# A long-convolution and linear-memory attention kernel on one core: another stored order of the same operations, with other PSUM banks and eviction engines

## The chip, the core and the metric

The kernel runs on one core of a Trainium2 chip. The core has a matrix engine (PE, which loads weights on a path of its own, PEld), a vector engine (DVE), a scalar engine (ACT), GpSimd (POOL), and a sync engine (SP) that here only issues transfers. PE writes its results to PSUM, eight banks of 512 fp32 columns on 128 partitions; DVE or ACT must evict them to the on-chip memory before a bank is used again. Each engine takes its instructions strictly in the order in which the program lists them, and waits where an operand isn't ready. The metric is the device time of one execution in microseconds (us), less is better.

## What is computed

Two layers that share nothing but the launch; their results are joined along the last axis (2048 x 1280).

```python
# A: a four-tap filter on k, times v, then a causal convolution over 2048 steps (by FFT), times q
k_shift = sum of k_pad[:, t:t + S] * shift_k[:, ks - 1 - t]
kv = k_shift * v
y  = irfft(rfft(kv, 4096) * rfft(ssm_k, 4096))[:S] + kv * ssm_D
a  = q * y
# B: 32 heads of 20, four segments of 512 steps, causal softmax inside a segment and a linear memory across
q, k, v = x @ wq, x @ wk, x @ wv
for s in range(4):
    a_dot = softmax(qs @ ks.T * scale + mask) @ vs
    a_mem = (phi(qs) @ M) / (phi(qs) @ z + 1e-6)
    o = g * a_mem + (1 - g) * a_dot
    M, z = M + phi(ks).T @ vs, z + sum(phi(ks))
b = o @ wo
```

## The kernel before

Layer A is cut into five blocks of 128 channels (`conv(dp)`). For each block the filter `ssm_k` and the product `kv` are brought into layout, taken through a discrete Fourier transform by matmuls with the table `Wf` (`spectrum`: eight PSUM groups "FK" for the filter and eight "FX" for kv), combined and multiplied on DVE (`product`, tiles F, Kh, Xh, pq, Y), and taken back by matmuls with `Wi` (`inverse`). The four taps are matmuls too, with diagonal weight tiles `skd`, 20 small products that ACT makes once from the `taps`. Layer B runs in eight units u: a segment s = u // 2 and a half of the heads. `project(u)` makes keys and queries (KQ, groups "P") and values (Va, groups "V") with the weights `wqkv`, transposes them by DMA into KQT, and bounds the scores (kam, A, qabs, and four "rows" transfers). `attend(u)` makes score tiles in PSUM ("S": A, D and J for the parts of the causal triangle, D the diagonal one), evicts them with an Exp on ACT into one of seven tiles ET, multiplies them by the values ("O") and normalises on DVE (rr, o2, o_s). `project_out(s)` multiplies by `wo` and stores. x's first segment is loaded in four quarters (Y_97 in the program's names) that PE transposes ("xt") into xT; the later segments are transposed by DMA. Ten warm-up matmuls on zeros stand first on PE.

None of this runs in the order of the code. A recorder (`Recorder`) takes each call as an operation with its predecessors: 1505 operations, 471 PSUM groups. `issue` then sends them out in the order of a stored table `ORDER`; `BASE` gives each group its first bank, and `EVICT`, a string of 227 digits, says for each plain eviction whether DVE ("1") or ACT ("0") does it (`evict`). So three tables decide what stands on each engine's list, and which bank a matmul waits for; nothing is scheduled at build time. All instructions are sent out from one line, L261, so the profile tells them apart by their tiles.

SP issues 201 transfers, GpSimd four (the constants `pack`, `shift_k`, `beta` and `ssm_D`).

Of the kernel before, what the change touches and what calls it, by code (L numbers as in the profile page):

```python
# [21 lines left out]
S = 2048; D = 640  # L22
H = 32; DH = 20; NS = 4; L = 512
# [246 lines left out]
class Layer:  # L270
# [134 lines left out]
    def evict(self, out, in_, grp):  # L405
        e = self.evicts
        self.evicts += 1
        if EVICT[e] == "1":
            self.nc.vector.tensor_copy(out=out, in_=in_, grp=grp)
# [506 lines left out]
    def project_out(self, s):  # L916
# [41 lines left out]
        for t in range(4):  # L958
# [31 lines left out]
SKA = (0, 1, 2, 3, 4)  # L990
KQV, QN = 0, 4
TAP2 = (3, 4)
EVICT = ("10100001110000001000000010000000000000000000000000000000000000100000000000001000010001001010100110100000000000000000110000000000000010000000"
         "000000000101000100100100000000000000010000001100001000000000000000000000010110010000100")
KQW, FW, WW = 1, 1, 1
ORDER = r"""
c-jrtgMttW5Czb=Gk0=rwrjI(+um&3wry{=YqM?Jwr#$5zT#w+Y?57aNKVNmxh0R}l_(NXTtrGs6^SI}q@v`L>Jn9=NgOF7p(MXlmGV+nk_aWQR+7{bAQdE|RFeV{Sqe%KEhI&?uv8XEKCPs6rKXsuRMxIiTWU#W
Ni5MNro@oa8cWJ(eyt%v(p?H@LP;gXw2qY3G*Vw`YC~x*^`x9;k=D{uifcCs(gxB<+DZ!vEw!|<l$177TboKh=^^bTtyIx;Qc-(J9c?9bwU0EBdfH6VOM5A$9i^(ql_FAH3Tl6;p*^Lr_LjcVLCWhO=_CWBn8cG|
l3cpT2<a@brG(Vi1d>RGNJA|u4K%C_mN7C=hRY~PDPd%s43)7mTB>OyEupJ*yo{6yQb>b!gErRcx<}S%d?~3-wTaHry|PjlX$tA4$t076lL|UfR%vscB$H)|?2`~(tW#yPY?AI;N@mDL-7l?lnrzbPazK`751p$s
rL`{AHabt6X<PlJEwsHJm6qB;=W9EiC0pg7bkd&MOBZNIJtlp1wj7qux=jwrHr=jAq__6bwc16y>Kxgj+hv^|my6O*Pe`!r)M2_=FUeI|p$m1m_SY>sK(EPMiDM&lr^K~gx>YaBX_+VEb-rAYcy>mX%Pxs(6Lp|2  # L1000
kli{#<J%57FN1WCuGif%Mx$A38>fq8uP&6NwnZ+;GTo<R^{gzG!MaSA>p3~5`!%Jdv7tIdPs&n>k5rb-qT6vjpp$f(PS;a1QV(i)nXEDFzKqsUn%Ex7bD5$`WQNYv>oQeu$qKn4H|4e**2j{>?#L{CDR<?NX0{`m
!B)#reIT<n0UpU~c_nM)jjWVJc2QqQR768Uq_DTLN)jQXWwQ11L@wz&$zoUZvOblha!sE}R@)$JB{9-lcDt&lb)CGIVV1)_N-`uzY&)w@bhw?-50V5S@>DlUPCKE`^ppl7DRS8-IjK`@gq_o=Hqr)KbX?FBh#<H1
yymvg5(9ZHrp2<<_#$bM#|GIqiHSS<Q19wjNrUV9NMqr#-q4$x4!884=CeMCjkkJVze|35pg&~1^|v^9r|<QZCbzU!!0yQ}iHiZ26|XhWe##roh<JFeza^bzLT3Dx43f>p+8>!<FSMY&)C86dAM}g<laKmU$5=uO
g-@CVpS7fY(}_0DfYO#8-!(J@KeUu(fFV03SxV$U8B2wqTGkZPtgscbB38+!8&S?8ps4jjWgBJ1tcp1zA}2;$aVuf7E!YNIE_A{Wt7>5|%Vt;}6h}3yZecOgCR+*Au-qt$APa|@79Qm-5{hAt<;7g9VEIrUg;5rz
QPE0bp1ri%))xVoZ-G+BDxe(dS`jR?0jOuStPB=eJ1d3yRuBQ~U_&iG8rV8pZ0)VJ^+!WnZ(t!Tu`rCxwicUhOxeOJVyO*8SjJ%#4na$+gk`qeMxd2d!3vAYMm7kQF%-iv5-V+i4Mt;YYE8`eTZf}6R#`QWG1=V4
U>us+Sj6H6tAUL+9^n`n9j%jvXJ-qs1YB)vY^`;%C@@RNuJ%{E8LczA+g9sg|Fox7M=$Gb+pLd?ZMXRB&P42Mn=A<va|$+FKXZ#j*cR)CP!@xCFqFG3G?TI)doTinFpSB$$EKn`yJG_O+78=i1+d?0;(-0piHOKR
*2Y1L#va&ZJFN@i@{mPmEhOU^i^qHDz&^Z-!`2gZ(3L58&d%B;>&trR#*`d|RJ>xBZ5q<B7mnHt)W<P9V#n=-rDjLY#7V1*(Ku!2tv9Bl0WMlZYY68gq-AKkV4>I*H!K~S;-=lQ!3?nG7{c2Y+3uKHW8AgLxM%Hn
)goDYUbFjXg!IhJ>z0uN*pv5dEHiOAnxGj@+hWYZ1AAnT?THQIQ=5%B2xFr-kip2pUR;9VoQs9%#0;E=wFqmYxdJ1&2wC~edb2Yh+Ip<R7`8)pF2xf(w`^R7hse!w+<<3zfc6;Ayd24ie2Ud*fjnG^HCTm7e2yG!
gPhF8`MANB$j1c;L4HnV7q-F_w#6k}Mr%x^djW>>f}GAG6feZ0gim8(7Go6Kh#7og#aW4=eI{REGfJ>BH=zpuvLv^lBevotI-mx__&5Gz5P$GHtFk74avQ4gJxg-}w__H|uq?~*Bdhb3T|q6DVtIbx96rJhd}19|
U@))ZG3K&1>vA?Dcmp<MBhF(*?!+}T<~O`S6E<aie!(vMVLgVk>-dhhXvRg{jfNi4!`oMUwi{^97Hr8@T+Hykg!8!vk-Rl;;<bITM*h*%7jgk3`&Yh#`7N~JC+x#gwq<*#f3nwjhbSK8x3Qe-xEB#@89R7XU(cGp  # L1010
9~&6L6?~7+*vMn}fK{yJoA?o{xsnI4mSH`bH}i0Q5NmiGwLQAOvwdvt@9hWnv%VkTQT)Ua1b7VJ%q`r?ZQRZV9@7uwAY=I<9O7ZN^&Q;FuNK=|czoZ@Jv@QE{DseK=dN-5H;(Wx{@@D(^dwsPQ6A$dgwns3*#F_p
{}GDkyLcM^40?)@HHp8qq#oDLK((uzez4O#i{tF#)Dt|zvka>z+0D-}wAS-5dY(NziiX#4n!qD!R6U2D9zoCJ7ZZ6Tji$-`0u%ZV>*W{O*?%*-CikBf=$CkzSD3<6`EN_<S9y(ptc~aQ>x`+ry^mi+L2v3Yw6Ul5
0^ZNRSsG90!t|cOGkR=|rD^@UHSs*2*ZX=t&*c5Rm1p(=UdV5<h+n`XX7y~I-Q#Kw&*FtWr^nG>*4m5uV?N+*=JMiR!i)Js-r^v?!%{xPOM4kF>*YM2j`Nb9+XwmtkFR%G-k-375BBl?ibMS#6KW;D&(}<#!@aUs
@$O#HhxrJv>Q7n66KN8y<|BQSKjUamtj}53$9Q$`=t;GcPxRC})?aXnPxVRulGA*;FZap*hRJk>ukac^(--<m-|ve(xz6@rpW}1=Ef4q-Po=Ybk*CzXo>7;28lC6!eV?!O6q-|)`38T-OuF7fe4{V$O&+MZbd_)R
b-u+9`XNuN>2$T{(af4&*Z5Z7=2>;S@9=E8(|7r9&!C5Wk00@io<(!(ZNKD4J-Z(B9D2s@_+7u}_x-G&^YebeFZ&h0>eu|b-|(A$%a8jBKk29ZwEqW|<?eI
"""
BASE = r"""
c-mc30kQ=l2qH7P|Bb%^HT(YTw3QJeIRFd<sz+jRy?dN_c64=g_q;oTp3i@FZ1$>p9(|HVZ-8vexIrYy61*|F0uj5v$#^nzP{qkt%qZ3%W{_Dok{Dq(H71#r0akn%z}00Jclvx$gQ@^)TGSeh?zfxH6-23;AWyw`
GIDlB{xWvhS!ov&h=r?#|M|G__KO;hF6kM(S=4$QIhkND<bo948P26xGGo5nVNc4hxwzjS4d5wUc|FGXSBGkq=gZwN=<DsC!5i{ii1N6e#&bEJpTGK5VbBdR*N<D$R8}UvVRi9&tDtL19a6U4NyYE>db(@z-nc&e
zj<yB_0_Fy+ZU-_pF7vVd_53;{d!F5fS_B_eBS8~RvQK@  # L1020
"""


# [69 lines left out]
```

## Time and profile before

| | us |
|---|---|
| runs before, median of 3 | 269.18 (268.61 to 269.23) |
| profiled execution, its span (the only time of it that the page has) | 266.3 |
| mean granted TensorE clock, share of full | 1.000 |
| moved by DMA | 41.84 MB, 157 GB/s on average |

A page of the profile shows one execution. Its parts used below are the busy time of each engine, the chain of work that ended last (followed back from the last instruction to what released it), groups of instructions by tile, and the list of instructions in order of time, merged where equal ones follow each other: start, length, engine, operation, output and input with their shapes, and in brackets the idle time before and what ended it. In the chain's list, each row is a start, a length, an engine and the tile written. An instruction's own length is longer than the distance to the next start on the same engine where they overlap.

### The profile page before, as it was taken

Reading aid. Unit: us, or ns where it says so; the run is one execution under the profiler, and the core shown is the slowest. Engines: PE = TensorE matmul, PEld = TensorE weight load, DVE = VectorE, ACT = ScalarE, POOL = GpSimd, SP = SyncE. Lnnn points to the kernel's source line nnn. Section 1 sums busy time; section 2 is a strip of 40 time slices with the busy share of each in tenths; the row PEclk is TensorE's granted clock in tenths of the full one; section 3 lists DMA queues with packets and bytes.
Section 4 is the critical chain, followed back from the end, with each engine's and each line's share of the span. In section 5 each row is a group of like instructions: output and inputs, shape, how many; then the busy total and the mean of one; then the engine's idle time right before and its main releaser. Section 6 shows DMA issues by size and latency. Waiting matters only on the chain.

```text
span 266.3 us, 10034 instructions
## 1 busy us (share of the span) xinstructions
PE 257.8 (97%) x4323; PEld 193.0 (72%) x4323; DVE 247.1 (93%) x387; ACT 248.8 (93%) x392; POOL 7.6 (3%) x20
## 2 busy tenths in 40 slices
PE   7999999999999999999999999999999999988994
PEld 3788678778777778877767777778776876665871
DVE  0599999999999999999999999999999999999971
ACT  2878999999999999999999999999999999999953
POOL 8300000000000000000000000000000000000000
PEclk9999999999999999999999999999999999999999
DMA  7999898999989797996999699958990099345034
GB/s 217 292 214 218 197 180 187 126 233 205 172 200 175 142 180 162 173 154 126 154 173 201 164 185 182 211 107 113 181 186 3 29 158 149 87 108 128 28 66 116
DMA packets 126604, 41.84 MB, mean 157 GB/s; under 512 B 114107, under 2 KB 125376, under 8 KB 126432
## 3 DMA queue, kind: packets, MB, share of 16 engines
q1 hardware_dynamic: 126416, 41.07, 80.1%
q8 instruction: 34, 0.56, 0.9%
q0 software_dynamic: 144, 0.13, 0.1%
q14 instruction: 10, 0.08, 0.1%
HBM read 11.96 MB, written 5.24 MB: 65 GB/s over the span
## 4 chain that ended last, share of the span: by engine, by line
PE 62%; ACT 28%; DVE 5%; issue 2%; DMA 1%; POOL 0%; DVEq 0%; ACTq 0%; POOLq 0%
PE ps L261 62%; ACT ET L261 19%; ACT F L261 3%; ACT KQ L261 1%; ACT PP L261 1%; DMA qabs<-in_A_shift_k_dram 1%; ACT Va L261 1%; DVE vt L261 1%; ACT outb L261 1%; DVE Y L261 1%; DVE Kh L261 1%; ACT qabs L261 1%; DVE pq L261 0%; ACT xT L261 0%; DVE o L261 0%
## 5 line engine op out<-in xcount | busy, mean ns | idle before, releaser
L261 ACT ACTIVATE ET<-ps 128x1024 bf16<-128x1024 f32 x160 | 162.6, 1122 | 0.4 <-PE ps L261 0.2
L261 PEld LDWEIGHTS <-xT 128*128 128x128 bf16 x640 | 57.3, 98 | 27.8 <-issue 6.8
L261 PE MATMUL ps<-wqkv,xT 128*128 128x320 bf16 x480 | 77.0, 299 | 0.4
L261 ACT CAST F<-ps 128x512 bf16<-128x512 f32 x72 | 43.3, 686 | 0.9 <-DVE F L261 0.8
L261 PE MATMUL ps<-Va,ET 128*128 128x21 bf16 x1280 | 41.8, 173 | 0.0
L261 PEld LDWEIGHTS <-ET 128*128 128x128 bf16 x1280 | 39.1, 96 | 2.1 <-issue 1.0
L261 PE MATMUL ps<-KQT 32*128 32x128 bf16 (+3 forms) x896 | 35.7, 239 | 0.3
L261 PEld LDWEIGHTS <-Wf 128*128 128x128 bf16 x320 | 29.8, 98 | 6.1 <-issue 1.3
L261 ACT CAST KQ<-ps 128x320 bf16<-128x320 f32 x54 | 25.5, 513 | 2.4 <-PE ps L261 2.3
L261 PE MATMUL ps<-wo,xT 128*128 128x320 bf16 (+2 forms) x160 | 25.5, 299 | 1.3 <-ACT ET L261 1.3
L261 PEld LDWEIGHTS <-KQT 32*128 32x128 bf16 (+1 forms) x896 | 16.1, 92 | 9.9 <-issue 8.2
L261 PE MATMUL ps<-kT,Wf 128*128 128x256 bf16 x160 | 21.8, 273 | 0.1
L261 PE MATMUL ps<-vt,Wf 128*128 128x256 bf16 x160 | 21.2, 273 | 0.0
L261 PE MATMUL ps<-Y,Wi 128*128 128x256 bf16 x160 | 20.8, 273 | 0.0
L261 DVE TENSOR_TENSOR o<-ps,rr 128x640 bf16<-128x640 f32 x24 | 19.7, 819 | 0.4
L261 DVE TENSOR_TENSOR Y<-Y,pq 128x2048 bf16<-128x2048 bf16 (+1 forms) x20 | 18.6, 937 | 0.0
L261 PE MATMUL ps<-Mbd,PqT 128*128 128x84 bf16 x96 | 18.3, 203 | 0.1
L261 DVE TENSOR_TENSOR pq<-Xh,Kh 128x2048 bf16<-128x2048 bf16 x15 | 18.2, 1215 | 0.0
L261 PE MATMUL ps<-skd,kr 128*128 128x128 bf16 (+4 forms) x124 | 17.9, 270 | 0.0
L261 PEld LDWEIGHTS <-kr 128*128 128x128 bf16 x124 | 15.6, 147 | 2.5 <-issue 0.8
L261 PEld LDWEIGHTS <-Wi 128*128 128x128 bf16 x160 | 14.8, 98 | 2.5 <-issue 0.6
L261 ACT ACTIVATE PP<-KQ 128x1280 bf16<-128x1280 bf16 x12 | 15.9, 1361 | 0.0
(87 smaller groups left out, 355.6 us busy)
## 6 DMA issues: line engine op xcount, KB each, us to landing
vt<-in_A_v_dram SPq DMA_DIRECT2D x10, 256.0 KB
pq<-in_A_q_dram SPq DMA_DIRECT2D x10, 256.0 KB
kT<-kT SPq DMA_DIRECT2D x32, 64.0 KB
out_dram<-pq SPq DMA_DIRECT2D x8, 256.0 KB
out_dram<-outb SPq DMA_DIRECT2D x12, 160.0 KB
Wf<-c_wf SPq DMA_DIRECT2D x4, 256.0 KB
Wi<-c_wi SPq DMA_DIRECT2D x1, 1024.0 KB
kb<-kr SPq DMA_DIRECT2D x4, 256.0 KB
```

What stands on the lines that cost most here:

```text
L261: f(*[fix(a) for a in args], **{k: fix(v) for k, v in kw.items()})
```

## The change

The tables `ORDER` and `BASE` are replaced and 52 of the digits in `EVICT` flip. No operation, shape or transfer is added or removed.

```diff
-EVICT = ("10100001110000001000000010000000000000000000000000000000000000100000000000001000010001001010100110100000000000000000110000000000000010000000"
-         "000000000101000100100100000000000000010000001100001000000000000000000000010110010000100")
+EVICT = ("01111110100100010010010000000000000000000000000000000000000000000000000000000000001010010100100000110000000000000000010000000000000000100000"
+         "000000000010100110100100001000010010000000000000111000000000001000100100000100000001010")
```

Of the flipped evictions 28 go from ACT to DVE: of 512 columns 7 of F, 2 of kT and 2 of the last output rows (PP); of 320 columns 5 of KQ, 4 of Va and 5 of outb; and 3 of x's quarters (640). 24 go from DVE to ACT: of 512 columns 8 of F and one each of kT, PP, qabs and xT; of 320 columns 6 of KQ and 5 of outb; and the taps (40). 390 of the 471 groups get another first bank. On every engine most operations stand elsewhere. On SP the head of the list was the first weights (wk, first half), the identity and x's quarters 0, 3, 1, 2; it now is the identity, x's quarters 3, 1, 2, 0, and then the first weights; the filter of block 0 follows in both, and the pieces of Wf and the other weights change places behind it. GpSimd's four transfers keep their sequence at the front (pack, shift_k, beta, ssm_D); its fills around them change places.

Where the prediction speaks of the start, ACT's list is this. Before (ps is PSUM; skd the diagonal tiles; A and rr the two Exps of beta; kT the filter of block 0):

```order
L261 ACT_TABLE_LOAD
L261 ACTIVATE skd_75<-ident,taps 128x128
L261 CAST xT_95<-ps 128x5x128
L261 ACTIVATE skd_77<-pack,taps 128x64
L261 CAST xT_95<-ps 128x5x128
L261 ACTIVATE A_93<-ps 128x32
L261 ACTIVATE rr_94<-ps 128x32
L261 CAST xT_95<-ps 128x5x128
L261 CAST KQ<-ps 128x16x20
L261 CAST kT_99<-ps 128x2x2x128
```

ACT's list at the same place now, from the table load on:

```order
L261 ACT_TABLE_LOAD
L261 COPY taps<-ps 128x40
L261 ACTIVATE skd_77<-pack,taps 128x64
L261 ACTIVATE skd_78<-pack,taps 128x64
L261 ACTIVATE skd_76<-ident,taps 128x128
L261 ACTIVATE rr_94<-ps 128x32
L261 ACTIVATE skd_76<-ident,taps 128x128
L261 ACTIVATE A_93<-ps 128x32
L261 ACTIVATE skd_75<-ident,taps 128x128
L261 ACTIVATE skd_74<-ident,taps 128x128 x2
```

The taps have come to ACT, three of x's quarters have left it, and diagonal tiles stand in their place; 15 of the 20 are ahead of the first eviction of KQ, where two were.

DVE's list at the start, before (after the fill of the warm-up's zeros):

```order
L261 MEMSET o_72 128x320
L261 COPY taps<-ps 128x40
L261 CAST xT_95<-ps 128x5x128
L261 CAST KQ<-ps 128x16x20
L261 TENSOR_SCALAR rr_94<-A_93 128x32
L261 CAST KQ<-ps 128x16x20 x3
L261 CAST kT_99<-ps 128x2x2x128
L261 TENSOR_SCALAR qabs_67<-KQ 128x1280
```

DVE's list at the same place now:

```order
L261 MEMSET o_72 128x320
L261 CAST xT_95<-ps 128x5x128 x3
L261 TENSOR_SCALAR A_93<-rr_94 128x32
L261 TENSOR_SCALAR rr_94<-A_93 128x32
L261 CAST xT_95<-ps 128x5x128
L261 CAST KQ<-ps 128x16x20 x3
L261 CAST kT_99<-ps 128x2x2x128
L261 TENSOR_TENSOR Mbd_91<-rr_94,pack 128x16
```

All four quarters of x are evicted here, three of them before anything else.

The third place is in the middle, on ACT, around the second diagonal score tile of unit 3 (ET6_115). Before:

```order
L261 CAST outb1_69<-ps_61 128x320
L261 ACTIVATE ET4_113<-ps_61 128x1024 x2
L261 ACTIVATE PP_80<-KQ_79 128x64x20
L261 ACTIVATE ET3_112<-ps_61 128x1024 x2
L261 CAST outb0_68<-ps_61 128x320
L261 CAST KQ_79<-ps_61 128x16x20 x2
L261 ACTIVATE ET6_115<-ps_61 128x1024 x2
L261 CAST F0_100<-ps_61 128x512
```

And now, on the same engine:

```order
L261 ACTIVATE ET4_113<-ps_61 128x1024 x2
L261 ACTIVATE PP_80<-KQ_79 128x64x20
L261 ACTIVATE ET3_112<-ps_61 128x1024
L261 CAST KQ_79<-ps_61 128x16x20
L261 ACTIVATE ET3_112<-ps_61 128x1024
L261 CAST outb1_69<-ps_61 128x320 x2
L261 CAST KQ_79<-ps_61 128x16x20
L261 CAST outb0_68<-ps_61 128x320
L261 ACTIVATE ET6_115<-ps_61 128x1024 x2
L261 CAST F0_100<-ps_61 128x512
```

Another output eviction (outb1) stands between the Exps here, 0.3 us more; on PE one more projection group stands ahead of the matmuls of ET6_115 (three projections of unit 5 instead of two).

More of the change, by code (lines that the diff above doesn't have):

````diff
@@ L995 @@
 KQW, FW, WW = 1, 1, 1
 ORDER = r"""
-c-jrtgMttW5Czb=Gk0=rwrjI(+um&3wry{=YqM?Jwr#$5zT#w+Y?57aNKVNmxh0R}l_(NXTtrGs6^SI}q@v`L>Jn9=NgOF7p(MXlmGV+nk_aWQR+7{bAQdE|RFeV{Sqe%KEhI&?uv8XEKCPs6rKXsuRMxIiTWU#W
-Ni5MNro@oa8cWJ(eyt%v(p?H@LP;gXw2qY3G*Vw`YC~x*^`x9;k=D{uifcCs(gxB<+DZ!vEw!|<l$177TboKh=^^bTtyIx;Qc-(J9c?9bwU0EBdfH6VOM5A$9i^(ql_FAH3Tl6;p*^Lr_LjcVLCWhO=_CWBn8cG|
-l3cpT2<a@brG(Vi1d>RGNJA|u4K%C_mN7C=hRY~PDPd%s43)7mTB>OyEupJ*yo{6yQb>b!gErRcx<}S%d?~3-wTaHry|PjlX$tA4$t076lL|UfR%vscB$H)|?2`~(tW#yPY?AI;N@mDL-7l?lnrzbPazK`751p$s
@@ L1000 @@
[L1000 to L1012, printed above, removed]
@@ L1013 @@
-0^ZNRSsG90!t|cOGkR=|rD^@UHSs*2*ZX=t&*c5Rm1p(=UdV5<h+n`XX7y~I-Q#Kw&*FtWr^nG>*4m5uV?N+*=JMiR!i)Js-r^v?!%{xPOM4kF>*YM2j`Nb9+XwmtkFR%G-k-375BBl?ibMS#6KW;D&(}<#!@aUs
-@$O#HhxrJv>Q7n66KN8y<|BQSKjUamtj}53$9Q$`=t;GcPxRC})?aXnPxVRulGA*;FZap*hRJk>ukac^(--<m-|ve(xz6@rpW}1=Ef4q-Po=Ybk*CzXo>7;28lC6!eV?!O6q-|)`38T-OuF7fe4{V$O&+MZbd_)R
-b-u+9`XNuN>2$T{(af4&*Z5Z7=2>;S@9=E8(|7r9&!C5Wk00@io<(!(ZNKD4J-Z(B9D2s@_+7u}_x-G&^YebeFZ&h0>eu|b-|(A$%a8jBKk29ZwEqW|<?eI
+c-jTQ17HvU6a>(_kF;zr+qP}DY}>YN+t#veEZes2_o4vEiYmy4?8t$fh=5$kjXcPUh=_!8$cL(^hNy^!q)3K}D1bmjMk*9Se56Ks6htM&Mt+n=ER;cXI8vel%AyF0qmslyUWtjqsE&B33_%)XL?%?06euG3L=lAA
@@ new lines @@
+NQ}D3j0DJnv`B{%C@Qs33^h;+HBnmXAQb9>D2f;;BaP7%K~hr;&CvwS&;nJYC0d~*8lsleM<Y~~*651b(iU~34H}@V6qEEwj{MRC?T`rNq&-5TBRZfPdZ9b|AR&rNUFnUU=!<?RA^lNL3P>k(K@tqZ5X41ijKe6D
+lo~PuV^C3sqp*xdeHn_eXdvS;5(6*@)nqURqM($Lh7uO#B@7x#b=ix?Qb?9cQ<;Ftn22CmCKY6}tdX@c2~#lz)3H$&%O;tI8CW9SWFLCS0W^{BGDi*~9JXLTW}=nMl@`)k7D!uZBMYUaw3BACN>)pInT2EMAV)Ay
+j-$DBlpWGZHsdJz%6yrPo^lACrI#GWO8F(drH{<THrXzhu~WKA7g;A4u}A{2Ui!%iT)`!5#~kdEVKNUV(O(A07TGNeFkD8+Hf)uFvPaI~DmKVj#L;Uwk3kYw=VQDqL_EEKy)sdDW1mFTomh+s5?{|@4;EpJMAMbn
+fw8h&Qfm?o!3x<g<K%#x!a*4<OOZyGU>T0fA=!%MNU5ihNOxhVtiTBwA_;jN(KVHhl>11khb4w4;3_268@P#ExPzA%Ef4V)qhy*)mq{{NrpOGLDM#c19^*ES$x+Fm8TBsS;VI%XDqmr$1nMI^M<#uOXIO)KSdACR
@@ new lines @@
+tg|E<v*<-xiw#JjvGp}B%NxYtYzgEQ$*LQ1NfI%;uERAsBeD4&>2*Dl@*{@nRXHayxd~@wxIU41%%LOn6EYwfgYi^8V5BDJNqHu5m{U*56ivbCoT|ArF~1<UhDaZtmd}W(c{B+J>UqhgX?a0nX*#CnLwO|E<r{8D
+8h*uNxh;A1j)ccuxhI)<Q*KEX4$|+)r}w2V^XpqFs6UXA4`jT)m!Ehi1vC@;Yb?H!3Hn-+X>y&WzwjGx<Sz<qT1}_fIbEO208OATB%$`>KfIK<%*sC)t6yZCevq${jUVNcl+<sMlHa9}&e6}3gQc~UPSjMKq$D_0
+f5;duqh&QcjiLBcl)@rfR5P%gIzzLPhUX}az{;AF#k7isVSg6a8Je3Vbg+hHRUNH)I8!?@7b7wfhiG1QW;HFZ)wPD!)WV#t6?Cpv)X7?$L0X<AIDqrCDD$y2%Q8P-YB>Iu`C5jvv=}R}whm+f7icXl$2wYsb#;-}
+({@^47i&qb*9O{N3v!8;Vh1h6$c$u5HL|tVo@}cdw4uhf?(9NZSB9}=+D2Ds9IMD)Y@wC7T*WFgtS!`5I)W`V3Wu-?hcb$-)Tq`-M{<=m)<GQ1CR&xNbr_p!OlzjY*<9CZHL8u_8jWQe)od&~>L#thP8!2H>pJbC
@@ new lines @@
+Q`l95bsWQ4LJMu(bSeW(bv(CeHzu$iY8v0VYeeg*f!0fVYaiXNiLI~p;9u!(J2a7P*6K`RLk+q```Iwts;<=D+@t^G4trRCOJ+5>Uk_*~J*bCtpC-2;PT(c()qWb@cB<%MEx?I9qM<c{)#h%!%v~DIj%r-%W6>?1
+oz=cpizzHbQ(6bB!>*Rf&gmuXW*w~_NAZ{**DHEiPiS49)M>oSQ+i(0*l14YMLn%<Gx$eB*(65L`b=#zc|p_KI;OLT+JHCo9+TQ_y`y*ao;GJgp3!E!rHy!BBk2Qu$fj&(57?MDHL_0TRc&wAb+9#IW_zeZtfyVm
+6&!1$?2*pmeLmJKwurNt!7|wseX6}|CBtY~oy&~2gv*%T7IO}t>2Moh^Et?(=yHy>5w?``IMO=Va~)`7EUUHS2CiopTgc9q%~o-owdVq6xAC@-Yq*+ExR$x?Df3z$Yr$vCVH2$lCs|AOw&%=gxoi{jSpl1DZJFO%
+@rJdgdnmunDRzYg?S&SxsaDvE8hpB4<uof~TR6jlS<H%CC8L+HnO4O@`(L}o>#S_oxS2Ot(q8bNZDkGnW?{S|Yg&-K<ahgFRjss@v9h*}9a!C}St;AWa`xUn*hl+mpX`;+we2i#wXA~e<UFfwbF7X%;$zOT`F4{H
@@ new lines @@
+tf4is*;dyYTLgc@30Bd<dp-MOZ`s7cX;b@ZUl^eEZLuw}rS@5OF}ybPX4c4?+iTs!ul%AdtfhV9ZU*=Qi|F6Em#wU|MfOPkifwG6ebhx3#oL;AR9|MF^fi~8d3%4yPu$NHR@3)UeZ6h44j$y6`JM;3(Kgvi3+t<F
+wMFx<8f=^G1H*ZAkLhbHhJR!&UuU)b5DzkzueJU5PTy;6Kg#25=3DFs57-ID^@DbVTP=<s<2KuFJFK}Mvics+e{!d_@WVW84g84hvbNsRe{qlf)powu{&Jt4<Uc)X@%=Qr`f>Yg$Lth$+ZRjZzj=ml^bf<zKSIJu
+Vo&0c<Sb9vTm7JsrHh}oGe$XSF6Y?UPgyrVYv(MKgjf%cAQ2@%&Rcj1Em0(l^mLV|lE6(wqDcsUS)iY1LjR$?{I^}Odj3<B`bE2Bm+gur_hcSju38Fj>TUd*UEps`<@r6Pr1b07+y7_`Dd-n@)B1P;Z|qGRmfF*L
+Ur*<0JiTY|jGo8)c`S)7{XLU^)4V>wziU3v>~W;K|I$L<%Cq<*%j&H?n-}ry{@8N(Ei3AUJ+9>RTt3+2$!#m<CA_#lu##Td2l)_xXz^vBm+`V*&hJ=mPax$zp_K9pKF%ljc)x3b^2(mrJsax7{Iyl`ik?{RTV=1}
@@ L1016 @@
+RlS;5_e3(>M|d5t;i;vrkMyUOMv}-VAMMZVxpnkTKGrAt7@y)V?4?chX+GJL$|RreD}0sD@HckAXL>SO<STu)zqNzD#25P<pX>8{sW10bvd`!HeorYGWtK1S<g(7+*)m`6DP)6ZlAMx7a>+)|ESo&H<dI<C><fL1
+ulB66)zeBgS?f7uyRY$da>%#&4&Uj!{D|-NJ-*iu`)$u4*ZioT^<#eAPxwi{?x*~;pYssUF6rft-}N(o-Y@t)zwbBvreE|+e#<ZW6~F5L0sLC-bN
 """
 BASE = r"""
-c-mc30kQ=l2qH7P|Bb%^HT(YTw3QJeIRFd<sz+jRy?dN_c64=g_q;oTp3i@FZ1$>p9(|HVZ-8vexIrYy61*|F0uj5v$#^nzP{qkt%qZ3%W{_Dok{Dq(H71#r0akn%z}00Jclvx$gQ@^)TGSeh?zfxH6-23;AWyw`
-GIDlB{xWvhS!ov&h=r?#|M|G__KO;hF6kM(S=4$QIhkND<bo948P26xGGo5nVNc4hxwzjS4d5wUc|FGXSBGkq=gZwN=<DsC!5i{ii1N6e#&bEJpTGK5VbBdR*N<D$R8}UvVRi9&tDtL19a6U4NyYE>db(@z-nc&e
@@ L1020 @@
-zj<yB_0_Fy+ZU-_pF7vVd_53;{d!F5fS_B_eBS8~RvQK@
+c-l>q3zo$o2tyJ1?0?5&FVQ!rr?x7Dkf@p4wz4o|^z&WTXU)$%ndO-^5$miqD{<D0x6jPU`=agqB|EOTW;F08qt0IN+8YgY2fc_W);9b$6`C3!;>T<eU#eO#>=)N$B`e=I;Z^5<>J>dTz0XbvzhM*SNpeS*g4gXi
+;P^2J@m+Mg&hCP3D=MkJL7rNhYWC1Z`Ba@jwl{wGqtf&fQa<F1v%AR)G{5~VVuyvvos`m}?2<|@>`k3Q-|NuekGmx%{&tM-#tEnTXmwR?@ot@<K!a4=dc6<+)!U?Gf?Rkq4yUq5mF6)puby*~=k#rLUSc1QagrZm
+ZqKn6tLweXkw8&@cci4r&n=f{<G>b%shcGBs#ov6-T6IZx1RmGi5K%@{0G!N1=;
 """
````

## The prediction

> **What bounds the kernel now.** First the page: busy shares and the chain of waits.
>
> ```profile
> PE 257.8 (97%) x4323; PEld 193.0 (72%) x4323; DVE 247.1 (93%) x387; ACT 248.8 (93%) x392; POOL 7.6 (3%) x20
> ...
> PE 62%; ACT 28%; DVE 5%; issue 2%; DMA 1%; POOL 0%; DVEq 0%; ACTq 0%; POOLq 0%
> ```
>
> Three engines are nearly full, and the chain changes hands between them. Next the busy time by stretches (length, then us of PE, PEld, DVE, ACT and POOL, granted clock, DMA share, GB/s):
>
> ```profile
> 10.00:20.00 10.00, 10.00 (x93) 8.47 (x92) 8.64 (x18) 7.37 (x17) 0.00 (x0) 1.00 1.05 242
> 20.00:30.00 10.00, 10.00 (x86) 7.85 (x85) 9.83 (x16) 8.67 (x25) 0.00 (x0) 1.00 1.04 227
> 30.00:50.00 20.00, 20.00 (x353) 15.37 (x351) 19.97 (x28) 19.89 (x34) 0.00 (x0) 1.00 0.87 164
> 50.00:100.00 50.00, 49.69 (x823) 37.49 (x822) 49.45 (x71) 49.97 (x79) 0.00 (x0) 1.00 0.99 184
> 100.00:150.00 50.00, 49.95 (x875) 37.92 (x874) 49.85 (x81) 50.00 (x78) 0.00 (x0) 1.00 0.91 164
> 150.00:200.00 50.00, 50.00 (x897) 37.95 (x896) 49.82 (x82) 49.90 (x77) 0.00 (x0) 1.00 0.94 166
> 200.00:250.00 50.00, 47.56 (x948) 34.34 (x945) 49.52 (x80) 50.00 (x69) 0.00 (x0) 1.00 0.47 92
> ```
>
> From 30 to 250 us ACT is busy 19.89 + 49.97 + 50.00 + 49.90 + 50.00 = 219.76 of 220 us, DVE 218.61. PE's figure says less, since its ends are modelled, but its load row falls from 37.95 to 34.34 in the last 50 us: there it waits for others. So **ACT carries the middle and DVE is close behind**. Slack is left only before 30 us, where ACT is busy 7.37 and 8.67 of ten. Third, the chain in order of time:
>
> ```profile
> 6.82 0.59 ACT xT L261
> ...
> 7.45 44.03 PE ps L261 x556
> ...
> 63.60 2.28 ACT F L261 x5
> ...
> 72.14 0.32 ACT KQ L261
> 72.46 1.85 ACT ET L261 x2
> ...
> 121.94 0.40 DVE KQ L261
> ```
>
> From 7.45 us, the first projection, PE holds the chain for 44 us; then ACT's evictions hold it in turns.
>
> **What the evictions cost.** 28 move from ACT to DVE and 24 the other way. Net, ACT gains one of 512 columns and one of 40 (the taps) and loses three of 320 and three of 640 (x's transposes); DVE has the opposite. ACT's prices in a full queue, from the chain: 2.28 / 5 = 0.46 to 0.48 for 512, 0.32 for 320, 0.59 for 640. DVE's, with its early rows (start, length):
>
> ```profile
> 6.18 0.20 DVE L261 COPY taps<-ps 128x40 f32<-128x40 f32 x1 [4.98 <-PE ps L261]
> 7.34 0.82 DVE L261 CAST xT<-ps 128x640 bf16<-128x640 f32 x1 [0.96 <-PE ps L261]
> ...
> 14.76 0.68 DVE L261 CAST F<-ps 128x512 bf16<-128x512 f32 x1
> 15.36 0.82 DVE L261 TENSOR_TENSOR PP<-PP,qabs 128x1280 bf16<-128x1280 bf16 x1
> ...
> 18.17 1.22 DVE L261 TENSOR_TENSOR Kh<-F 128x2048 bf16<-128x2048 bf16 x1
> ...
> 27.77 1.23 DVE L261 TENSOR_TENSOR Xh<-F 128x2048 bf16<-128x2048 bf16 x1
> ```
>
> 0.60 for 512 (14.76 to 15.36), 0.40 for 320 (the chain), and for 640 the 0.82 less the 0.08 by which 0.68 shrinks in a queue: 0.75, an estimate. So ACT: +0.48 - 3 x 0.32 - 3 x 0.59 + 0.1 = **-2.2 us**. DVE: -0.60 + 3 x 0.40 + 3 x 0.75 - 0.1 = **+2.7 us**. PE: nothing; it has the same matmuls.
>
> The Trainium skill ("VectorE: DVE Perf Modes", section "The TRN2 errata — SBUF-src ops pay a fixed extra latency per instruction") gives an eviction from PSUM 120 cycles plus its columns at 0.96 GHz on VectorE and 172 plus its columns at 1.2 GHz on ScalarE. By that the sums would be about -2.5 and +2.9, estimates from the page. The DVE rows' lengths agree (0.68 and 0.82 against 0.66 and 0.79), but the next start comes 0.08 sooner.
>
> **The start, engine by engine.** PE's rows there, and ACT's:
>
> ```profile
> 1.26 3.59 PE L261 MATMUL ps<-o 128*128 128x512 bf16 x9 [1.26 <-DVE o L261]
> 5.52 0.62 PE L261 MATMUL ps<-ident,qabs 5*64 5x5 bf16 x12 [0.67 <-DMA qabs<-in_A_shift_k_dram]
> 6.08 0.45 PE L261 MATMUL ps<-ident,Y 128*128 128x128 bf16 x5
> 6.37 0.38 PE L261 MATMUL ps<-o 128*128 128x512 bf16 x1
> 6.58 0.72 PE L261 MATMUL ps<-ident,Y 128*128 128x128 bf16 x10
> 7.45 0.85 PE L261 MATMUL ps<-wqkv,xT 128*128 128x320 bf16 x5
> 8.14 0.44 PE L261 MATMUL ps<-ident,Y 128*128 128x128 bf16 x5
> 8.52 0.18 PE L261 MATMUL ps<-outb,ident 1*128 1x32 bf16 x1
> ...
> 17.30 1.93 PE L261 MATMUL ps<-skd,kr 128*128 128x512 bf16 x14
> ...
> 23.09 3.66 PE L261 MATMUL ps<-vt,Wf 128*128 128x256 bf16 x32
> ...
> 31.86 0.38 PE L261 MATMUL ps<-pack 32*128 32x128 bf16 x16
> ```
>
> ```profile
> 11.17 0.35 ACT L261 ACTIVATE skd<-pack,taps 128x64 bf16<-128x64 bf16 x1
> ...
> 33.73 1.96 ACT L261 ACTIVATE ET<-ps 128x1024 bf16<-128x1024 f32 x2
> ```
>
> PE: x's third quarter is now turned in the hole between warm-up (1.26 + 3.59) and taps, which still wait for GpSimd's shift_k, 5.52. After the taps (6.08) come beta 0.11, two quarters at 0.29 (6.08 to 6.37), a warm-up 0.21 (6.37 to 6.58) and the last quarter: the first projection at **7.27**, if its weights are there. The second waits for DVE, which now evicts all quarters in a row (about 6.5 to 7.3, then to 8.1): 0.25 lost. From the first projection to the X spectrum PE needed 23.09 - 7.45 = 15.64; now without a quarter (0.38), beta (0.11) and one value projection (0.68; the first took 7.45 to 8.14), plus 0.25, 14.72: it begins at 22.0. With that projection still owed, before's 23.09 counts as 22.41: PE is 0.4 ahead. The first score tile stood at 31.86; 22.0 + 8.77 + the 0.68 owed, less some 0.2 of small waits between its groups, is 31.3: 0.55 ahead.
>
> DVE: its K combine needs ACT's last K eviction. PE's K groups ended at 17.30, 9.85 after the first projection; two of seven key and query projections are now behind them, so 7.27 + 9.85 - 0.49 - 2 x 0.68 + 0.25 = 15.5, and ACT, with two evictions of 0.48 left, ends the last near 16.4. So the combine starts at 16.45, not 18.17. From there to the X combine the old order takes 27.77 - 18.17 = 9.60; the new one has one F eviction more (0.60), one small operation and some idle less (0.25): 26.4 instead of 27.77, **1.37 ahead**. Up to that point it has done 3 x 0.75 (x) + 0.60 (kT) + 0.60 (F) - 0.40 (KQ) + 0.12 - 0.1 = 3.1 us more, so of its +2.7 there is -0.4 left: in terms of work left, DVE is some 1.75 us ahead.
>
> ACT: most of the 20 diagonal tiles now stand right behind the taps, where ACT idled. Up to the first Exp of the first full score tile it has 1.8 us less (-3 x 0.59 - 0.48 for kT - 0.48 for F + 0.32 for KQ + 0.1 for the taps + two small diagonals at some 0.24, their 0.35 less the overlap); of the -2.2 about -0.35 is left. That Exp is the second of the row at 33.73, so 34.65. Now it follows the first score tile (31.3, 0.55 long, 0.1 to start), two Exps of 0.92 (half of 1.85) and one KQ: 34.1. So **ACT is 0.55 + 0.35 = 0.9 ahead**.
>
> **The middle and the end.** After 35 us the remaining work is the same to within 0.4 us on each engine, in another mixture. The end holds the same matmuls on PE, and one eviction and one store stand last as before: nothing. The sum is the lead of the engine that has no slack, ACT: **-0.9 us**. The profiled execution spans 266.3; the median of the runs is 269.18, so 2.9 us lie around the span. 265.4 + 2.9 = **268.3**.
>
> **The rivals.**
>
> 1. *The new order makes ACT wait (slower).* The place: the second diagonal tile of attention unit 3, near 132 us.
>
> ```profile
> 131.86 0.64 PE L261 MATMUL ps<-pack 32*128 32x128 bf16 x15
> ...
> 132.67 1.53 PE L261 MATMUL ps<-wqkv,xT 128*128 128x320 bf16 x10
> ```
>
> ```profile
> 132.82 2.08 ACT L261 ACTIVATE ET<-ps 128x1024 bf16<-128x1024 f32 x2
> ```
>
> PE now has one projection more ahead of that tile (0.68, half of 1.53 less its tail), so with its lead of 0.55 it begins at 132.0 and ends near 132.6. ACT came to its Exp at 132.82 from a full queue; with its lead of 0.9, less 0.3 because 0.3 us more of its work now stands in front, it asks at 132.2 and waits 0.4. One such wait leaves half the gain, two none. From 30 to 250 us ACT idled 0.24 us in all, so each is new; with five (268.3 + 2.0 = 270.3) the kernel is measurably slower, and six give 270.7. For it: 390 of 471 bank choices are new, and every engine's list is mixed anew. Against: PE could be pulled along by the earlier evictions.
>
> 2. *The lead is eaten (no change).* One to four such waits and nothing gained from DVE: 268.7 to 269.9.
>
> 3. *DVE's lead counts too (faster).* Where the chain stood on DVE, as at 121.94, its 1.75 us is what PE and ACT waited for: 267.4.
>
> 4. *The first weights come late (no change).* They were SP's first transfer and are now its sixth:
>
> ```profile
> 0.74 0.45 SPq L261 DMA_DIRECT2D wqkv<-in_B_wk_dram  x1
> 1.24 0.51 SPq L261 DMA_DIRECT2D ident<-c_ident  x1
> 1.79 1.85 SPq L261 DMA_DIRECT2D Y<-in_B_x_dram  x4
> ```
>
> SP's landings are not shown. Issued at about 3.1 instead of 0.74, they cost nothing if they land by 7.27. From above: the same six transfers stood first before, and the last of them was in use at 8.14, so 8.14 bounds the new order too: PE then loses 0.87, more than its lead, and ACT's goes with it: 269.2.
>
> **How the numbers follow.** ACT's lead kept, 268.3 (267.8 to 268.6): 0.34. DVE's lead counts, 267.4 and down to 266.6 if PE's waits in the last 50 us close with it: 0.12. Lead eaten: 0.20. Weights late: 0.08. ACT waits five times or more: 0.26. One measurement tells 0.3% (0.8 us) from no change, so faster is under 268.4 and slower over 270.0. Faster: 0.30 of the first case and the 0.12, 0.42. Same: 0.04 + 0.20 + 0.08 = 0.32. Slower: 0.26. For eight in ten I take 266.6 to 270.7, the DVE case to six waits; a better or worse order than that stays outside.
>
> **What would show it.** The first projection near 7.2 us and the first X spectrum near 22.0 on PE; the X combine near 26.4 on DVE; ACT's busy time from 30 to 250 still above 219. If ACT's idle in that stretch grows to a microsecond or more, released by PE, rival 1 holds. If the first projection starts near 8, rival 4 holds. A chain with more DVE than 5% would say that the 2.7 us put on DVE matter, and the forecast would be wrong.

## The result, and the profile after

| | before | after |
|---|---|---|
| runs, median (lowest to highest), us | 268.53 (267.95 to 269.87), 8 runs | 270.61 (269.73 to 276.39), 8 runs |
| profiled execution, span, us | 266.3 | 268.3 |

The changed kernel takes 1.0076 times as long (95% interval 1.0047 to 1.0105): slower by some 2 us, where 268.3 was forecast. The run of 276.39, at a mean granted clock of 0.986, is not in the ratio. The profiled execution took 270.14 us. A second measurement of it, beside other kernels, gave 1.0119 (1.0089 to 1.0149), a median of 272.07 us and a span of 270.5.

First the page of the changed kernel: busy shares, and the chain of work that ended last.

```profile
PE 255.2 (95%) x4323; PEld 192.2 (72%) x4323; DVE 250.2 (93%) x391; ACT 248.0 (92%) x388; POOL 7.5 (3%) x20
...
PE 51%; ACT 16%; DVE 14%; DMA 10%; issue 6%; SPq 1%; POOL 0%; DVEq 0%; ACTq 0%; POOLq 0%
```

DVE has 3.1 us more to do and ACT 0.8 less (forecast: 2.7 and 2.2). In the chain, DMA has gone from 1% to 10% and DVE from 5% to 14%: transfers now stand on the path. Where the time went is read from windows (length, then busy us of PE, PEld, DVE, ACT and POOL, granted clock, DMA share, GB/s). Before:

```profile
0.00:35.00 35.00, 32.93 (x303) 24.37 (x304) 25.19 (x44) 25.23 (x61) 7.59 (x20) 1.00 0.93 229
50.00:250.00 200.00, 197.20 (x3534) 147.69 (x3533) 198.64 (x310) 199.87 (x299) 0.00 (x0) 1.00 0.83 151
35.00:275.00 240.00, 224.91 (x4023) 168.67 (x4020) 221.93 (x344) 223.58 (x332) 0.00 (x0) 1.00 0.77 141
```

The same windows of the changed kernel, and one more:

```profile
0.00:35.00 35.00, 32.66 (x302) 23.91 (x303) 28.56 (x48) 23.72 (x60) 7.54 (x20) 1.00 0.96 225
50.00:100.00 50.00, 49.15 (x834) 37.25 (x823) 48.63 (x69) 50.00 (x77) 0.00 (x0) 1.00 1.09 174
50.00:250.00 200.00, 193.31 (x3507) 146.03 (x3496) 196.02 (x306) 198.69 (x294) 0.00 (x0) 1.00 0.85 147
35.00:275.00 240.00, 222.53 (x4025) 168.33 (x4022) 221.59 (x344) 224.29 (x330) 0.00 (x0) 0.99 0.80 141
```

The last row of each, from 35 us to the end, is the **work left** at 35 us. ACT, the engine without slack, has 224.29 - 223.58 = **0.71 us more** left than before; the forecast had it 0.9 ahead. From 50 to 250 us it then loses 199.87 - 198.69 = **1.18 us** to waits that weren't there. Together 1.89 of the 2.0 us by which the span grew. The work left counts busy time as it turned out, and an eviction behind a wait takes more of it: in the two kernels below with wo moved, whose lists are the changed kernel's own up to 70 us, ACT has 225.32 and 225.29 left, 1.7 us more than before. So the 0.71 is not the start's alone. DVE is the other way round at 35 us: 0.34 us less left, though the tables give it 3.1 more in all. So its added evictions were done early, in time that was idle; but from 50 to 250 us DVE loses 198.64 - 196.02 = 2.62 us.

**The start.** PE's instructions in order of time, changed kernel:

```profile
8.10 2.21 PE L261 MATMUL ps<-wqkv,xT 128*128 128x320 bf16 x15 [0.89 <-DVE xT L261]
...
22.56 3.66 PE L261 MATMUL ps<-vt,Wf 128*128 128x256 bf16 x32
...
32.09 0.38 PE L261 MATMUL ps<-pack 32*128 32x128 bf16 x16
```

Its list of waits, one row (engine, what it waited for, us in total, times, longest):

```profile
PEld L261 <- DMA wqkv<-in_B_wk_dram: 1.1, 1, 1.1
```

The first projection starts at 8.10, not 7.27. The bracket names DVE, whose eviction (7.24, 0.83 long) ended as the weights came, but the row of waits says that the weight load stood 1.1 us for them; in the run with light weights (below) PE does not wait for that eviction. From there the lag runs through: the X spectrum at 22.56 (forecast 22.0), the first score tile at 32.09 (31.3; before 31.86). On DVE:

```profile
16.90 1.22 DVE L261 TENSOR_TENSOR Kh<-F 128x2048 bf16<-128x2048 bf16 x1 [0.36 <-ACT F L261]
...
27.46 1.22 DVE L261 TENSOR_TENSOR Xh<-F 128x2048 bf16<-128x2048 bf16 x1
...
92.92 0.49 DVE L261 TENSOR_SCALAR qabs<-KQ 128x1280 bf16<-128x1280 bf16 x1 [0.49 <-DMA KQT<-qabs]
...
100.42 0.69 DVE L261 TENSOR_TENSOR pq<-ps,pq 128x512 bf16<-128x512 f32 x1 [0.98 <-DMA pq<-in_A_q_dram]
...
132.84 0.49 DVE L261 CAST KQ<-ps 128x320 bf16<-128x320 f32 x1 [0.52 <-DMA KQT<-KQ]
...
239.41 0.49 DVE L261 CAST outb<-ps 128x320 bf16<-128x320 f32 x1 [0.69 <-DMA out_dram<-outb]
```

**The middle.** The last four rows are new: each time DVE, whose list is strict, stands for a transfer, 0.49 + 0.98 + 0.52 + 0.69 = 2.7 us, the whole of its loss of 2.62. Before, no row of DVE, ACT or PE between 30 and 250 us named a transfer. The wait at 100 us is handed on to PE and from there to ACT:

```profile
101.16 1.03 PE L261 MATMUL ps<-Y,Wi 128*128 128x256 bf16 x8 [1.10 <-DVE pq L261]
```

```profile
102.91 0.43 ACT L261 CAST Va<-ps 128x320 bf16<-128x320 f32 x1 [0.48 <-PE ps L261]
103.59 0.43 ACT L261 CAST Va<-ps 128x320 bf16<-128x320 f32 x1 [0.25 <-PE ps L261]
```

These two are 0.73 of ACT's 1.18. The chain (start, length, engine and tile) shows the same stretch from the other end:

```profile
83.01 7.95 DMA wo<-in_B_wo_dram
90.98 1.82 DMA KQT<-qabs
...
95.74 4.55 DMA pq<-in_A_q_dram
...
127.78 4.97 DMA KQT<-KQ
```

And SP, which issues them (lengths are those of the issue):

```profile
83.01 0.95 SPq L261 DMA_DIRECT2D wo<-in_B_wo_dram  x1
...
84.77 1.34 SPq L261 DMA_DIRECT2D KQT<-qabs  x2
...
90.98 0.54 SPq L261 DMA_DIRECT2D KQT<-qabs  x1
91.93 2.69 SPq L261 DMA_TRANSPOSE KQT<-KQ  x2
94.72 1.81 SPq L261 DMA_DIRECT2D pq<-in_A_q_dram  x2
```

wo, 800 KB, stands ahead of the small rows of unit 2 and of q. SP itself stood for 2.4 us, until 90.98, for wo to land. The trace says why: SP's transfers take eight landing semaphores in turn, and the eighth one behind wo, which is the last row of unit 2, takes wo's own, so it is not issued before wo has landed (90.96). Once issued it landed in 1.8 us (92.80). When each transfer landed, worked out from the semaphore events of the trace, against the first instruction that needs it (spare time in brackets, us):

```
transfer                          before                  after
wk, first half                    4.21 / 7.45   (3.24)    8.05 / 8.10     (0.05)
last row of unit 2                96.75 / 100.79 (4.04)   92.80 / 92.92   (0.12)
second q of block 1               96.61 / 99.05  (2.44)   100.29 / 100.42 (0.12)
last KQT transpose of unit 4      131.44 / 132.19 (0.76)  132.75 / 132.84 (0.09)
store that frees an outb tile     234.10 / 236.17 (2.07)  239.28 / 239.41 (0.12)
```

A spare time of 0.1 us is a wait: the instruction starts as soon as the data is seen. The new order asks for the rows 7.9 us earlier than before, and they land only 3.9 us earlier. Of the store, 15 of 16 parts had landed by 237.45; the last came 1.8 us later, for a reason that was not found.

### The profile page after: what moved, and what is told of

It is laid out like the page before. It is cut to its first block, busy times and chain, and to the rows that moved or that the text cites. A ratio compares the mean times of both kernels' runs of the same rounds, so it can differ in the third digit from the quotient of the medians.

```text
span 268.3 us, 10060 instructions
## 1 busy us (share of the span) xinstructions
PE 255.2 (95%) x4323; PEld 192.2 (72%) x4323; DVE 250.2 (93%) x391; ACT 248.0 (92%) x388; POOL 7.5 (3%) x20
## 4 chain that ended last, share of the span: by engine, by line
PE 51%; ACT 16%; DVE 14%; DMA 10%; issue 6%; SPq 1%; POOL 0%; DVEq 0%; ACTq 0%; POOLq 0%
PE ps L261 51%; ACT ET L261 10%; DVE Xh L261 4%; DMA wo<-in_B_wo_dram 3%; DVE Y L261 2%; ACT F L261 2%; DMA KQT<-KQ 2%; DMA pq<-in_A_q_dram 2%; DVE o L261 2%; ACT KQ L261 2%; DMA out_dram<-outb 1%; DMA KQT<-qabs 1%; DMA outb<-in_B_beta_dram 1%; DVE pq L261 1%; DVE qabs L261 1%
## 5 line engine op out<-in xcount | busy, mean ns | idle before, releaser
L261 PEld LDWEIGHTS <-xT 128*128 128x128 bf16 x640 | 58.2, 98 | 29.1 <-issue 6.5
L261 PE MATMUL ps<-wqkv,xT 128*128 128x320 bf16 x480 | 75.9, 300 | 1.2 <-DVE xT L261 0.9
L261 PE MATMUL ps<-KQT 32*128 32x128 bf16 (+3 forms) x896 | 32.8, 239 | 0.6 <-DVE o L261 0.4
L261 PE MATMUL ps<-vt,Wf 128*128 128x256 bf16 x160 | 22.0, 272 | 0.3 <-ACT qabs L261 0.2
L261 PEld LDWEIGHTS <-KQT 32*128 32x128 bf16 (+1 forms) x896 | 15.2, 92 | 9.0 <-issue 7.7
L261 PE MATMUL ps<-kT,Wf 128*128 128x256 bf16 x160 | 21.0, 273 | 0.0
L261 ACT CAST Va<-ps 128x320 bf16<-128x320 f32 x27 | 13.1, 494 | 4.0 <-PE ps L261 4.0
```

The lines of the kernel that those rows point to most:

```text
L261: f(*[fix(a) for a in args], **{k: fix(v) for k, v in kw.items()})
```

## The experiments

Four theories. **T**: the transfers that come late in the middle cost the time. **W**: the first weights, behind x and the identity, cost it. **E**: DVE's extra evictions cost it. **P**: PE's order and banks do, whatever the transfers. Unless said otherwise the kernels are the changed one with one edit; ratios are to the kernel before, timed alongside, with 95% intervals.

### Moving one transfer

SP's list, wo later (behind q):

```diff
-DMA wo<-in_B_wo_dram 128x5x640
 DMA kb<-kr
...
 DMA pq_104<-in_A_q_dram x2
+DMA wo<-in_B_wo_dram 128x5x640
```

> The changed kernel with one row moved on SP: the load of wo (800 KB) stands behind the two loads of q for block 1 instead of ahead of the rows of unit 2, some 13 us later. Theory T (late transfers): DVE's waits for the rows of unit 2 (0.49 us at 92.4) and for q of block 1 (0.98 at 99.4) go, and with them ACT's 0.7 at 102.4, as PE no longer waits there; the time falls by about 1.0 us, to 269.6 where the kernel before is 268.5 and the changed one 270.6. Rival E (the 2.7 us of evictions put on DVE): no wait on the path goes, the time stays within 0.3 us of 270.6. Rival P (PE's order and banks): 270.6 too.

Measured: 274.31 us, 1.0197 (1.016 to 1.0234). The waits at 92 and 100 us are gone, and a longer one stands elsewhere on DVE:

```profile
117.62 0.69 DVE L261 TENSOR_SCALAR qabs<-KQT 128x2048 int16<-128x2048 int16 x1 [2.52 <-DMA KQT<-KQ]
```

wo earlier (between two pairs of a filter transfer and a store):

```diff
 DMA kT_99<-kT_98
+DMA wo<-in_B_wo_dram 128x5x640
 DMA out_dram<-pq_104
```

> The changed kernel with the load of wo ahead of the last pieces of block 2's filter, some 8.5 us earlier on SP, near the place it has in the kernel before. Theory T: as with wo behind q, 1.0 us less, unless the big load delays k of block 3 and the transposes right behind it by its own 5 us and DVE waits there instead. Rivals E and P: 270.6 within 0.3.

Measured: 274.05 us, 1.0196 (1.016 to 1.0232). Here a store comes late, and with it the tile that it frees. PE stood 2.53 us behind it, and then the granted clock was 0.5 from 87.44 to 90.85, which is part of this run's loss:

```profile
84.49 1.23 DVE L261 TENSOR_TENSOR pq<-Xh,Kh 128x2048 bf16<-128x2048 bf16 x1 [3.03 <-DMA out_dram<-pq]
```

So T's simple form fails: the late transfers are not one slip. The DMA share is 1.09 from 50 to 100 us (0.99 before), and with wo moved either way another transfer came late.

q of block 1 ahead of two transposes:

```diff
+DMA pq_104<-in_A_q_dram 128x8x128 x2
 DMA_TRANSPOSE KQT_86<-KQ x2
...
-DMA pq_104<-in_A_q_dram 128x8x128 x2
```

> The changed kernel with the two loads of q of block 1 ahead of the transposes KT of unit 3 on SP; nothing left out. Theory T: the loads are issued at about 92.5 instead of 94.7, land before 98.5, DVE's wait of 0.98 to 1.8 at 99 to 101 and ACT's behind it vanish, and no other wait grows: 0.7 to 1.2 us less than the changed kernel, 1.003 to 1.006. If the DMA queue and not SP's sequence is what delays them, the wait shrinks by less than 0.4 us and the time by as little.

Measured: 271.26 us, 1.0089 (1.0056 to 1.0122), not told apart from the changed kernel. The wait at 100 us is gone, but ACT lost 199.87 - 199.08 = 0.79 us between 50 and 250 us, 0.68 of it in one new wait. (The clock was at 0.5 from 8.64 to 12.05 us in this execution, so its start and span can't be compared.)

```profile
125.88 1.94 ACT L261 ACTIVATE ET<-ps 128x1024 bf16<-128x1024 f32 x2 [0.68 <-PE ps L261]
```

The first weights at the head of SP's list, as before:

```diff
+DMA wqkv<-in_B_wk_dram 128x5x320
 DMA ident<-c_ident
 DMA Y_97<-in_B_x_dram x4
-DMA wqkv<-in_B_wk_dram 128x5x320
```

> The changed kernel with the first half of wk as SP's first transfer again (x's quarters and the identity move back by one). Theory W (the weights' place at the head of SP's list took the start's lead): the first projection at 7.3 to 7.5 us instead of 8.10, the first full score tile's Exp some 0.7 earlier than 34.87, and the time 0.7 less, 269.9. Rival (the start has slack behind it, or x's quarters now come later by as much): the first projection still near 8, or early with the time at 270.6 within 0.3.

Measured: 272.12 us, 1.0103 (1.0062 to 1.0143), no gain. PE's start shows why: x's first quarter is now late instead (it starts at 4.52 in the changed kernel), and the projection no earlier.

```profile
5.69 0.62 PE L261 MATMUL ps<-ident,Y 128*128 128x128 bf16 x5 [0.41 <-DMA Y<-in_B_x_dram]
...
8.21 2.33 PE L261 MATMUL ps<-wqkv,xT 128*128 128x320 bf16 x15
```

### Undoing one list

The old EVICT with the new ORDER and BASE:

```diff
-EVICT = (after)
+EVICT = (before)
```

> The changed kernel's order and banks with the eviction engines of the kernel before: all 52 digits flipped back, each eviction at its new place in the order. Rival E (the evictions are the cost): DVE's 2.7 us of work go back to ACT (2.2), DVE is no longer what ends last, and the time is near 268.5. Theory T: the transfers stand where they stood, DVE's waits at 92, 99 and 132 stay, the time is 270 to 271.5 (the start is worse by up to 0.9, since x's quarters go back to ACT behind the diagonal tiles).

Measured: 288.41 us, 1.0757 (1.0713 to 1.0802). Each engine's list then waits for the other's in many places, so nothing follows for E.

The new lists with SP's list of before:

```diff
-SP: after's 201 transfers in their order
+SP: the same transfers in before's order
```

> The changed kernel's PE, ACT, DVE and GpSimd lists, banks and eviction engines, with SP's whole list of the kernel before. Theory T in its strong form (the loss is SP's list alone): DVE's waits for transfers go and the time is 268 to 269, that of the kernel before. Weak form (SP's list and the engines' lists only work together; each list is fitted to its own): new waits for transfers elsewhere, slower than the changed kernel. Rivals E and P: about 270.6, no wait that matters changes.

Measured: 288.74 us, 1.0746 (1.071 to 1.0782). The largest of its waits is for the same rows as above, eleven times as long (the granted clock then falls to 0.5 from 110.68 to 117.51):

```profile
107.13 0.49 DVE L261 TENSOR_SCALAR qabs<-KQ 128x1280 bf16<-128x1280 bf16 x1 [5.45 <-DMA KQT<-qabs]
```

The lists of the engines and of SP belong together. Neither run can price a part of the change.

### Making a transfer light

The better test leaves every list as it is and shortens a transfer. One fifth of wo is loaded, and used five times (so B's output projection has wrong weights); the same edit goes into the kernel before.

```diff
-nc.sync.dma_start(out=self.wo[:], in_=B_wo.rearrange(...))
+nc.sync.dma_start(out=self.wo[:, 0:1], in_=B_wo.rearrange(...)[:, 0:1])
...
-rhs=self.wo[:, cc, 0:512]
+rhs=self.wo[:, 0, 0:512]
```

> The changed kernel, every instruction in its place, but wo's load brings one fifth of it (160 KB instead of 800 KB) and the output projections use that fifth five times; so only the transfers behind it get sooner. Theory T: DVE's waits for the rows of unit 2 (0.49 at 92.4) and for q of block 1 (0.98 at 99.4) vanish, with ACT's 0.7 at 102.4 behind them, and nothing else is later; the time falls by 0.9 to 1.5 us, to about 1.003 to 1.004 of the kernel before, where the changed kernel stood at 1.0076. Rivals E and P: within 0.3 us of the changed kernel.

> The same fifth of wo in the kernel before, as a control. Theory T: no transfer was late there, so nothing is won: the ratio is 1.000 within 0.0015. If it falls by as much as in the changed kernel, the load costs both the same and the change's loss is elsewhere.

Measured: 269.87 us, 1.0049 (1.0027 to 1.0071) for the changed kernel; 1.0009 (0.9984 to 1.0033), nothing, for the kernel before. Its profiled execution can't be used (see the last section), so it was repeated beside the changed kernel itself, with two more: *light*, in which A's stores of blocks 0 to 3 move 32 of 128 partitions too (the rest of A's output is not written) and the output eviction that waited at 239 us has a tile of its own; and the same edits in the kernel before.

```diff
-out=rows, in_=qd[:, ...]
+out=rows[0:32], in_=qd[0:32, ...]
...
+if (s, t) == (2, 3):
+    outb = self.consts.tile([128, 2, 320], bf16, name="outbx")[:]
```

> The changed kernel itself, beside the three next ones on one chip. All theories: 1.0076 of the kernel before (1.005 to 1.0105); DVE's waits for transfers at 92, 99, 132 and 239 us add up to 2.7 us, within 0.5.

> The changed kernel with one fifth of wo loaded, again, for a readable profile. Theory T: the waits at 92 and 99 are gone and nothing is later; 0.5 to 1.3 us less than the changed kernel beside it. Rivals E and P: the waits may go, but the time stays within 0.3 us.

> The changed kernel's lists, banks and engines, with fewer bytes behind SP: a fifth of wo, a quarter of the rows of the A stores of blocks 0 to 3 (left out: the other rows), and a buffer of its own for the last outb of segment 2, which waits for a store at 239 us. Theory T (late transfers are the whole loss): DVE's marked waits for transfers after 80 us fall from 2.7 to under 0.8 us, ACT's behind them too, and the ratio to the kernel before falls to 1.000 to 1.002. Rivals E and P (evictions on DVE, PE's order): the ratio stays above 1.005 though the transfers come early.

> The same lighter transfers in the kernel before, as a control. Theory T: no engine waited for a transfer there, so 0.999 to 1.001. If it falls by as much as the changed kernel does, lighter transfers help any order and say nothing of the change.

Measured in one batch: changed 1.0119 (1.0089 to 1.0149), wo lightened 1.0051 (1.0028 to 1.0073), light 1.0050 (1.0023 to 1.0077), light before 1.0000 (0.9979 to 1.002). The intervals of the changed kernel and of the two light ones don't meet; 272.07 - 269.50 = 2.6 us in this batch. Against the first measurement, 1.0076, it is 0.7 us, and there the intervals overlap. So the late transfers cost **0.7 to 2.6 us**, and the lists before have none of it. The granted clock is part of that scatter: over the executions with a mean of 0.997 or more, the medians are 270.61 (10 of the changed kernel) and 269.50 (16 with wo lightened), **1.1 us** apart, an estimate across batches. The windows of the changed kernel, measured again:

```profile
50.00:250.00 200.00, 192.49 (x3492) 145.41 (x3482) 195.40 (x304) 198.09 (x294) 0.00 (x0) 1.00 0.84 146
35.00:275.00 240.00, 223.86 (x4026) 169.20 (x4025) 221.73 (x345) 224.63 (x330) 0.00 (x0) 0.99 0.79 142
250.00:255.00 5.00, 4.68 (x111) 3.46 (x108) 4.82 (x10) 4.17 (x6) 0.00 (x0) 0.71 0.11 36
```

DVE's waits for transfers are there again: 0.55, 1.76, 0.55 and 0.29 us. The brackets name ACT at the first two (93.19 and 101.47), but the row and q landed 0.12 us before each (93.07 and 101.35), as above.

Those with wo lightened:

```profile
50.00:250.00 200.00, 193.93 (x3556) 146.69 (x3556) 197.17 (x308) 199.54 (x295) 0.00 (x0) 1.00 0.81 144
35.00:275.00 240.00, 222.20 (x4026) 168.25 (x4025) 221.94 (x345) 224.48 (x330) 0.00 (x0) 1.00 0.77 139
```

ACT's loss between 50 and 250 us goes from 199.87 - 198.09 = 1.78 to 0.33. The work left at 35 us stays: 1.05 and 0.90 us more than before. Two of DVE's rows with wo lightened, and the second of them in *light*:

```profile
92.89 0.49 DVE L261 TENSOR_SCALAR qabs<-KQ 128x1280 bf16<-128x1280 bf16 x1
...
99.81 0.69 DVE L261 TENSOR_TENSOR pq<-ps,pq 128x512 bf16<-128x512 f32 x1 [0.40 <-ACT ET L261]
```

```profile
100.01 0.69 DVE L261 TENSOR_TENSOR pq<-ps,pq 128x512 bf16<-128x512 f32 x1 [0.48 <-DMA pq<-in_A_q_dram]
```

The rows come in time. q still doesn't, though the first bracket names ACT: its last part landed at 99.69, 0.12 us before the start (the other 15 by 98.25). The wait near 132 us stays too (0.85 and 0.53). DVE still has all its extra evictions, which speaks against E: with the same work on DVE, ACT's middle is nearly whole again.

W was tried in the same way: one fifth of wk's first half is loaded and used five times (keys wrong).

```diff
-wk, first half: 5 pieces of 128 rows
+wk, first half: 1 piece, used for all five
```

> The changed kernel with one fifth of the first half of wk loaded (82 KB instead of 410 KB), used five times; order untouched. Theory W (weights landing at 8.05 take the start's lead): the first projection starts at 7.25, all transfers behind land 1 to 1.5 us sooner, and the time falls by 0.8 us or more. Rival (the start is paced by something else too, e.g. DVE's four x evictions in a row, the next ends near 9): the first projection at 7.3 but the X spectrum still after 22.3 and the time within 0.3 us of the changed kernel.

Measured: 271.02 us, 1.0112 (1.009 to 1.0134), no gain. PE's rows:

```profile
7.06 2.42 PE L261 MATMUL ps<-wqkv,xT 128*128 128x320 bf16 x15
...
21.91 0.27 PE L261 MATMUL ps<-vt,Wf 128*128 128x256 bf16 x1
22.50 3.54 PE L261 MATMUL ps<-vt,Wf 128*128 128x256 bf16 x31 [0.33 <-DVE vt L261]
...
31.92 0.38 PE L261 MATMUL ps<-pack 32*128 32x128 bf16 x16
```

The first projection gains 1.04 us. The X spectrum's first matmul keeps 0.65 of it, but the other 31 wait for DVE's kv (vt), and the group ends 0.18 us earlier (26.04 instead of 26.22). So early weights alone don't bring the forecast's lead; W explains the first row, not the loss.

### Joining the two orders

Three kernels take the first operations from one order with their banks and evictions, and the rest from the other in its own sequence; the seam stands near 72 us (412 operations) or 180 us (973).

```diff
 ORDER, BASE, EVICT:
+start_of_after:  after's first 412 operations, then before's rest
+start_of_before: before's first 412 operations, then after's rest
+end_of_after:    before's first 973 operations, then after's rest
```

> The reverse: the first 412 operations as in the changed kernel, the others as before. By the work left at 69 us ACT is 0.7 us behind and DVE 0.4 ahead: 0.3 to 0.9 us slower than before, ratio 1.001 to 1.0035, no engine waiting for a transfer after 80 us. If the forecast's lead existed: faster, 0.9965. If the start carries all: 1.0075.

> The first 412 of the 1505 operations in the order, with the banks and the eviction engines of the kernel before (up to about 69 us), all others as in the changed kernel. If the start costs what ACT's work left says (0.7 us at 35 us) and the rest is lost later: 0.5 to 0.9 us less than the changed kernel, a ratio to the kernel before of 1.004 to 1.006, with DVE's waits for transfers at 92 and 99 still there. If the middle alone carries the loss: as the changed kernel, 1.0076 or more. If the start carries all of it: 1.000.

> The first 973 operations as before (to about 168 us), the others as in the changed kernel. By the work left the last third costs ACT 0.2 and DVE 0.7 us (the wait for outb's store at 239): ratio 1.000 to 1.002. If the end carries half of the loss: 1.004.

Measured: the changed start alone 1.0017 (0.9997 to 1.0036), 269.19 against 268.67 us; the changed middle and end 1.0137 (1.0096 to 1.0178); the changed end 1.0322 (1.0295 to 1.0349). The windows of the first:

```profile
50.00:250.00 200.00, 197.18 (x3560) 147.57 (x3558) 197.55 (x307) 199.87 (x299) 0.00 (x0) 1.00 0.82 148
35.00:275.00 240.00, 225.53 (x4034) 168.93 (x4034) 221.70 (x343) 224.50 (x333) 0.00 (x0) 0.99 0.78 142
```

It loses nothing in the middle, as before, and has 0.92 us more left on ACT at 35 us; its span is 267.3, 1.0 longer. By its times, a median of 0.5 us, the start costs **0 to 1 us**. The second has the wait for q as well, though it begins as before did:

```profile
101.94 0.69 DVE L261 TENSOR_TENSOR pq<-ps,pq 128x512 bf16<-128x512 f32 x1 [1.49 <-DMA pq<-in_A_q_dram]
```

So the middle waits for transfers with either start. The third has seams of its own, where a tile made by the one order is wanted sooner by the other, and behind them the granted clock is 0.5 from 184.66 to 194.90; it says nothing of the end:

```profile
186.49 1.27 ACT L261 ACTIVATE PP<-KQ 128x1280 bf16<-128x1280 bf16 x1 [5.22 <-DMA PqT<-PP]
```

Last, two kernels that should have come out even with before: *light* with q moved ahead, and *light* with before's first 412 operations.

```diff
+light_lq: light_after, and q ahead of the two transposes
+closed:   light_after, and before's first 412 operations, then after's rest
```

> The changed kernel with the lighter transfers (a fifth of wo, a quarter of the rows of the A stores of blocks 0 to 3, an own buffer for one outb) and the loads of q of block 1 ahead of two transposes. Theory T plus start: DVE's wait at 100 gone, only the 0.5 us for KQT at 132 left; ACT's work left grows by less than 0.3 us from 35 to 250 us (changed kernel: 1.2 to 1.8); ratio to the kernel before 1.002 to 1.004. Rivals E and P: still 1.005.

> The same with the first 412 operations of the kernel before. If start and transfers are all of the loss: 1.000 to 1.002, ACT's and DVE's work left within 0.5 us of the kernel before's from 75 us to the end (beside a late start of the execution itself). If something else in the changed middle costs time: 1.003 or more with no wait for a transfer to show for it.

Measured: 1.0064 (1.0033 to 1.0096) and 1.0097 (1.0064 to 1.013). Both miss. In the first no row of DVE or ACT between 30 and 250 us names a transfer any more, and yet it is no quicker than *light*; its profiled execution had a granted clock of 0.95 throughout, so its windows don't compare. The second began late (its start is in the last section), and lost one wait after its seam. Its windows and one row of ACT:

```profile
50.00:250.00 200.00, 193.74 (x3507) 146.31 (x3507) 197.94 (x309) 199.15 (x297) 0.00 (x0) 1.00 0.77 140
35.00:275.00 240.00, 223.42 (x4037) 169.37 (x4039) 224.00 (x348) 225.53 (x333) 0.00 (x0) 1.00 0.73 133
```

```profile
75.60 0.42 ACT L261 CAST KQ<-ps 128x320 bf16<-128x320 f32 x1 [0.58 <-PE ps L261]
```

ACT has 1.95 us more left at 35 us although the lists are those of before there, and 0.58 of the 0.72 us that it loses later is this wait, behind the seam. So the middle with light transfers and the old head loses little more than that in its profile, but its times contradict it: not one of its six runs is under 270.53. None of the kernels is faster than the kernel before.

## Why the prediction was wrong

The sign was wrong. 270.61 lies just inside the range, by luck: the upper end was put there for six waits of rival 1's kind, which did not occur. In spans, 265.4 was forecast and 268.3 measured. Of these 2.9 us, 1.61 are ACT's lead (0.9 ahead forecast, 0.71 behind measured) and 1.18 its waits in the middle.

- **The step that failed in the middle: "After 35 us the remaining work is the same to within 0.4 us on each engine, in another mixture."** The amount of work was off by less than a microsecond (DVE -0.34, ACT +0.71); what was left out is when its data comes. The sum has no term for SP's transfers behind the start, and no rival either. The runs showed four transfers with 0.1 us to spare where there were 0.8 to 4.0, 2.7 us of DVE's time for them, and 0.7 to 2.6 us of the kernel's time that goes when wo, the large transfer ahead of two of them, is made light.
- **The step that failed in the start: the lead of 0.9 us measured 0.71 behind**, and 0.9 to 1.7 behind in other executions that began with it at full clock. First, the first projection was at 8.10, not at 7.27: "if its weights are there" did not hold. The forecast carried this as rival 4 ("starts near 8"), rightly as to the mechanism. Its bound of 8.14 was met by chance: that was when the last quarter of x was used, but the quarter had landed by 6.81, while the same six transfers now take until 8.05. Second, the later steps don't hang on that alone, as the run with light weights showed: PE then waited for DVE's kv, and the first score tile came at 31.92, not 31.3. The K combine (16.90, forecast 16.45) and the X combine (27.46, forecast 26.4) are late too; with light weights they stood at 16.74 and 27.29, the K combine waiting 0.39 us for ACT's F. The first full score tile's Exp stood at 34.87, not 34.1 (before: 34.65):

```profile
34.87 1.97 ACT L261 ACTIVATE ET<-ps 128x1024 bf16<-128x1024 f32 x2
```

- **"ACT: -2.2 us" measured -0.8.** DVE's +2.7 measured +3.1. The prices were those of a full queue. An eviction that follows a wait overlaps no other, so its whole length counts: the two at 102.91 and 103.59 took 0.43 each, where 0.32, the distance to the next start, was put. That goes in the right direction; that it makes up all of the 1.4 us was not shown.
- **"2.9 us lie around the span"** measured 1.8: the execution of 270.14 us has a span of 268.3, and its seven other runs are 1.7 to 1.8 longer than their spans. The forecast set the median of three runs against the span of another, quicker execution, which made it 1.1 us too long; this is apart from the change.
- **Rival 1** was right in its sign: "if ACT's idle grows to a microsecond or more, released by PE", and it lost 1.18. Its place and mechanism were wrong. No wait stands near 132 us on ACT, and at 101 us PE waited for DVE's pq, which empties a bank, and DVE for q: neither PE's order nor the choice of banks was the origin. The releaser named in a bracket is one link; the cause stood two links further back.
- **"A chain with more DVE than 5% would say that the 2.7 us put on DVE matter."** It has 14%, yet the inference doesn't hold: DVE had its extra work done by 35 us, and stands in the chain because it waits for transfers.
- **Rivals 2 and 3**: the lead wasn't eaten by single waits, there was none; and DVE's lead at 35 us, 0.34 instead of 1.75, was worth nothing, since what DVE waited for was not work.

What stays open: the two parts don't add up within their scatter (0 to 1 for the start, 0.7 to 2.6 for transfers, against spans that grew by 2.0 and 4.2). With the transfers light, 1.0050, about 1.3 us, is left, of which the profiles put 0.9 on the start, but the kernel with the old head did not confirm it. P was not tested by itself, and the rest could be its. In the second measurement ACT also lost 0.83 and 0.82 us to PE in the last 20 us; there the granted clock was 0.71 from 250 to 255 us, and eight matmuls that took 1.03 us at 101.16 in the first took 1.87 at 252.10. So these 1.65 of the 4.2 us go with PE's clock, not with the lists. The wait of 0.69 us at 239 us was taken out only together with others. E is not supported, but no run took DVE's evictions away cleanly.

## What to carry to other kernels

When consumers move, set each transfer's landing against its first use before and after: with the DMA engines as full as here, four transfers did not follow the instructions that were moved ahead, and moving wo either way made another transfer late. Compare two kernels by the work that each engine has left at one moment; it parts what was lost by then from what is lost later, which shares of busy time don't, though evictions that later waits lengthen count into it. And follow a wait to the last releaser in the row before naming its cause, by the landing times where a bracket can name another engine.

## What the runs showed of the hardware

**A small transfer waits for a large one ahead of it.** A row transfer of 4 KB landed 1.7 us after its issue at 200.24 us, in a queue with nothing ahead, and 6.0 us after its issue at 84.77, behind wo; with a fifth of wo, the same row landed 2.7 us after its issue (85.56). SP issues all its transfers on one queue here. The Trainium skill ("DMA: Bandwidth & Descriptors", section "Two DMAs through the same engine are not ordered") says that descriptors in one queue of an engine start in order; these rows agree. SP itself stopped too, 2.4 us, because its next transfer was to use the landing semaphore that wo still held:

```profile
SPq L261 <- DMA wo<-in_B_wo_dram: 2.4, 1, 2.4
```

**A stretch of half clock, in pieces of 3.41 us.** The traces list the granted clock. With wo earlier, PE stood 2.53 us until 86.37, and the clock is 0.5 from 87.44 to 90.85; with SP's list of before, it stood 4.96 us until 111.48, and the clock is 0.5 from 110.68 to 117.51, twice as long. But a wait of PE of 1.88 us until 102.22 in the changed kernel, measured again, was followed by none, and its stretch from 252.13 to 255.55 came behind waits of at most 0.32 us. Such a piece costs some 1.7 us: with the changed start alone, the execution with a mean clock of 0.991 took 270.83 us, the median of the eleven at 0.997 or more is 269.15.

**PE at half rate while the clock column reads 1.00.** The kernel with before's head and light transfers started like this:

```profile
7.96 1.54 PE L261 MATMUL ps<-wqkv,xT 128*128 128x320 bf16 x5
```

The same five matmuls took 0.85 us before. One execution of the kernel with light wo took 458.52 us, its others 268.7 to 271.22, and was left out of the ratio; in it a group that takes 0.83 us in the kernel above (at 72.89) looks like this:

```profile
69.57 1.61 PE L261 MATMUL ps<-skd,kr 128*128 128x384 bf16 x6 [0.28 <-issue]
```

Its mean clock is given as 1.000 as well. The column counts 1.00 wherever the trace has no record of the clock: the first one is at 10.70 us in the kernel with before's head (at 4.29 in the kernel before), and the execution of 458.52 us has none. The Trainium skill ("TensorE: Matmul & The Clock Gate", section "What's actually happening") has an idle state at half clock that ends after some 3.4 us of sustained work, by a window that runs freely; the record at 10.70 instead of 4.29 agrees with a window that ended later. Why one execution stayed at half rate was not found. Read the matmuls' lengths, not the clock alone.
